# The seam between an inverse transform and a gated feed-forward: moving one transpose and one small transform, and moving one PSUM copy from ScalarE to VectorE

## The chip, the cores and the metric

The kernel runs on one core of one Trainium2 chip. The metric is device time in microseconds (us). Each execution also has a profiled span, from the first to the last instruction, which is about 1.8 us shorter. TensorE multiplies matrices into PSUM, which this kernel uses as 8 banks of 512 fp32 values per partition; ScalarE (ACT) and VectorE (DVE) move results from PSUM to SBUF ("evict" them; in the traces here 128x578 took 0.66 us on ScalarE); GpSimd (POOL) and SyncE (SP) start the transfers here, and GpSimd also computes ahead of the feed-forward (39.1 us busy in all, the DMA issues included).

## The reference

```python
def _A_ref(x, w_r, w_i):                     # spectral filter
    X = rfft2(x.astype(float32), axes=(-2, -1))
    y = irfft2(X * (w_r + 1j * w_i), s=(S, D), axes=(-2, -1)).astype(bfloat16)
    return y

def _B_ref(x, w_gate, w_up, w_down):         # gated feed-forward
    return (gelu(x @ w_gate) * (x @ w_up)) @ w_down

h  = x + _A_ref(layernorm(x), w_r, w_i)      # x: 1 x 2048 x 576, bf16
h2 = h + _B_ref(layernorm(h), w_gate, w_up, w_down)   # 576 -> 4608 -> 576
```

## The kernel before

The 2048 tokens are 16 tiles of 128. The Fourier transforms are matmuls with tables. The stage that matters is the last of the inverse transform and the start of the feed-forward. I name its pieces by token tile c:

- **I(c)**: six matmuls of 289 columns (three per PSUM bank, two banks), then the eviction into `GS`.
- **N(c)**: four matmuls of 288 columns, the last inverse transform; VectorE then adds the residual and sums the row for the next layernorm.
- **turn(k)**: the feed-forward wants the normalized tokens of the first block (tiles 0 to 3) with features on partitions. TensorE transposes each tile with five 128-column matmuls against an identity into two PSUM banks; one copy of 640 columns takes it to `HT0`.
- **gate/up**: 2592 matmuls of 512 columns that contract over only 64 rows (I call these half-height; all the others above are full-height, with 128 rows). They go in pairs, one on the upper and one on the lower half of the array, with the lower half six matmuls behind. The first six, `gu(0)`, therefore run alone; I call them the lone six. In the chain of waits of the kernel before, 648 paired ones take 70.05 us, 0.108 each, and the lone six 1.40, 0.233 each.

```python
TURN = (8, 10, 12, 14)            # after which tiles the four turns come

def islot(c):                     # I(c) uses PSUM banks 0,1 or 2,3
    return (c + sum(c > t for t in TURN)) % 2

def i_ev(c):
    sl, b0 = c % 2, 2 * islot(c)
    if c == 0:
        ...
    else:                         # one ScalarE instruction evicts both banks
        P.op(ACT, ... a.activation(GS[:, sl, :, 0:K2], banks(b0, 2, K2), ACTF.Copy),
             r=[("PS", b0), ("PS", b0 + 1)], w=[("G", sl, 0), ("G", sl, 1)])

def turn_pe(c):
    b0 = 2 * ((TURN[c] + 1 + c) % 2)        # the other pair of banks
    for k in range(5):
        ... PE matmul: HN tile x identity -> bank b0 + k // 4
    P.op(ACT, ... a.activation(HT0[:, 0:5, t0:t1], PS[... 640 columns from b0 ...], ACTF.Copy),
         r=[("PS", b0), ("PS", b0 + 1)], w=[("HT", 0, c, 0)])

st_I01()
for c in range(1, NT):
    if c >= 2:
        st_I(c)                   # six matmuls and i_ev(c)
    st_N(c - 1)
    ...                           # layernorm of tiles 0 to 3 at c = 5, 6, 7
    if c in TURN:
        turn_pe(TURN.index(c))
...
def gu(n):                        # gate/up, one step
    ...                           # n = 0: the lone six
    if n - 1 < 0:
        st_N(NT - 1)              # N15 comes inside the gate/up stream
        ...
```

A small scheduler in the kernel derives every semaphore wait from the `r` and `w` keys. A turn takes the pair of banks that would have been next, so the tile after a turn, I(c+1), uses the *same* banks as I(c). The kernel gives each engine its instructions as one list, in program order.

## Time and profile before

| | before |
|---|---|
| time, median of 3 first runs | 504.44 us (504.13 to 504.98) |
| profiled span | 502.9 us |
| TensorE busy | 98% |
| gate/up in the chain of waits | 56% |
| down projection in the chain of waits | 28% |

These are the first line of the engine table and the two lines of the chain on the profile's page. The chain follows the work that ended last back from the end; the shares are of the span.

```profile
PE 492.4 (98%) x4318; PEld 297.7 (59%) x4319; DVE 183.9 (37%) x391; ACT 158.7 (32%) x296; POOL 39.1 (8%) x49
...
PE 91%; DVE 6%; issue 1%; DMA 1%; ACT 1%; DVEq 0%
PE PS L838 56%; PE PS L861 28%; PE PS L700 3%; DVE TP L629 2%; PE PS L739 2%; PE PS L600 1%; DVE ST L440 1%; DVE CUS L606 1%; PE PS L645 1%; DVE CUS L607 1%; DMA XO<-in_A_x_dram 1%; PE PS L620 1%; DVE U L505 0%; DVE ATS L472 0%; ACT JNK L431 0%
```

The kernel is bound by TensorE: it is busy for 98% of the span, at a mean granted clock of 1.000 in the trace, and 91% of the chain lies on it. Below is the chain of waits of the kernel before, in order of time, around the seam. The columns are: start in us, length in us, engine, what is written, source line, and count. L700 is I, L739 is N, L784 is a turn, L838 is gate/up, L861 is the down projection. The first line is I8, the last I ahead of the first turn. In the experiments' kernels the line numbers shift by a few with each edit: I stays L700, N is L739 or L742, a turn L784 or L787, gate/up lies between L838 and L848.

```profile
65.15 0.75 PE PS L700 x6
...
72.49 0.90 PE PS L700 x6
73.39 0.49 PE PS L739 x4
73.88 0.75 PE PS L700 x6
74.63 0.49 PE PS L739 x4
75.12 0.28 PE PS L784 x5
75.40 0.90 PE PS L700 x6
76.30 0.49 PE PS L739 x4
76.79 1.40 PE PS L838 x6
78.19 0.60 PE PS L739 x4
78.79 70.05 PE PS L838 x648
148.84 35.39 PE PS L861 x288
```

TensorE is on the chain at every moment here, yet the same six matmuls take 0.75 us in one place and 0.90 in another (I13 at 72.49 and I15 at 75.40, both after a turn), and the same four take 0.49 or 0.60 (N15, inside the gate/up stream). A "busy" TensorE hides small waits, because the records of successive matmuls overlap: in the down projection successive matmuls of 288 columns start 0.123 us apart (288 in 35.39) and are each recorded as 0.286 long.

The timeline of the kernel before shows the wait. Its columns are: start, length, engine, line, operation, tiles, shape, count, and in brackets the idle time before it with what ended that.

```profile
74.67 0.66 ACT L709 ACTIVATE GS<-PS 128x578 bf16<-128x578 f32 x1 [0.59 <-PE PS L700]
...
74.96 0.44 PE L784 MATMUL PS<-IDT,HN 128*128 128x128 bf16 x5
...
75.38 0.92 PE L700 MATMUL PS<-DT,V 128*128 128x289 bf16 x6
...
76.34 0.66 ACT L709 ACTIVATE GS<-PS 128x578 bf16<-128x578 f32 x1 [0.19 <-PE PS L700]
...
78.12 0.67 PE L739 MATMUL PS<-GS,IT 128*128 128x288 bf16 x4
```

ScalarE evicts I14 from 74.67 to 75.33, and I15 begins at 75.38, although the turn ahead of it needs only 0.28 us from 74.96. On the other side, I15's own eviction (76.34 to 77.00) is long over when N15 begins at 78.12: the lone six hide it.

### The profile page before, as it was taken

Reading aid. Unit: us, or ns where it says so; the run is one execution under the profiler, and the core shown is the slowest. Engines: PE = TensorE matmul, PEld = TensorE weight load, DVE = VectorE, ACT = ScalarE, POOL = GpSimd, SP = SyncE. Lnnn points to the kernel's source line nnn. Section 1 sums busy time; section 2 is a strip of 40 time slices with the busy share of each in tenths; the row PEclk is TensorE's granted clock in tenths of the full one; section 3 lists DMA queues with packets and bytes.
Section 4 is the critical chain, followed back from the end, with each engine's and each line's share of the span. In section 5 each row is a group of like instructions: output and inputs, shape, how many; then the busy total and the mean of one; then the engine's idle time right before and its main releaser. Section 6 shows DMA issues by size and latency. Waiting matters only on the chain.

```text
span 502.9 us, 9972 instructions
## 1 busy us (share of the span) xinstructions
PE 492.4 (98%) x4318; PEld 297.7 (59%) x4319; DVE 183.9 (37%) x391; ACT 158.7 (32%) x296; POOL 39.1 (8%) x49
## 2 busy tenths in 40 slices
PE   6899999999999999999999999999999999999998
PEld 2687674444458764444477744444577644444775
DVE  5899673344431114343310134333201233333111
ACT  7888776653220003333200023323100133323000
POOL 3644281000000000000000000000000000000000
PEclk9999999999999999999999999999999999999999
DMA  8779789001100000100000001100000000000000
GB/s 284 165 224 334 235 292 353 6 4 25 25 5 13 18 19 17 22 17 1 2 7 18 19 15 23 22 4 1 1 18 19 13 1 1 1 2 2 12 19 19
DMA packets 25948, 28.64 MB, mean 57 GB/s; under 512 B 11568, under 2 KB 19888, under 8 KB 25776
## 3 DMA queue, kind: packets, MB, share of 16 engines
q1 hardware_dynamic: 23328, 17.39, 12.1%
q0 software_dynamic: 2576, 10.62, 6.3%
q8 instruction: 34, 0.56, 0.5%
q14 instruction: 10, 0.08, 0.1%
HBM read 23.66 MB, written 2.36 MB: 52 GB/s over the span
## 4 chain that ended last, share of the span: by engine, by line
PE 91%; DVE 6%; issue 1%; DMA 1%; ACT 1%; DVEq 0%
PE PS L838 56%; PE PS L861 28%; PE PS L700 3%; DVE TP L629 2%; PE PS L739 2%; PE PS L600 1%; DVE ST L440 1%; DVE CUS L606 1%; PE PS L645 1%; DVE CUS L607 1%; DMA XO<-in_A_x_dram 1%; PE PS L620 1%; DVE U L505 0%; DVE ATS L472 0%; ACT JNK L431 0%
## 5 line engine op out<-in xcount | busy, mean ns | idle before, releaser
L838 PE MATMUL PS<-HT,WGU 64*128 64x512 bf16 x2592 | 281.9, 376 | 0.0
L838 PEld LDWEIGHTS PS<-HT,WGU 64*128 64x128 bf16 x2592 | 137.3, 94 | 143.4 <-issue 1.2
L850 ACT ACTIVATE GL<-PS 128x512 bf16<-128x512 f32 x144 | 85.9, 597 | 289.3 <-PE PS L838 289.3
L851 DVE TENSOR_TENSOR AT<-GL,PS 128x512 bf16<-128x512 bf16 x144 | 99.0, 688 | 174.1 <-PE PS L838 172.5
L861 PE MATMUL PS<-WD,AT 128*128 128x288 bf16 (+2 forms) x1152 | 141.8, 286 | 0.0
L861 PEld LDWEIGHTS PS<-WD,AT 128*128 128x128 bf16 x1152 | 111.0, 98 | 31.5 <-issue 1.7
L864 DVE TENSOR_TENSOR OS<-PS,XO 128x288 bf16<-128x288 f32 (+2 forms) x32 | 14.7, 458 | 125.8 <-PE PS L861 125.8
L665 POOL TENSOR_SCALAR WS<-WS 128x290 bf16<-128x290 bf16 x16 | 15.2, 949 | 9.3 <-DMA WS<-in_A_w_i_dram 8.2
L742 DVE SCALAR_TENSOR_TENSOR XO<-PS,XO 128x576 bf16<-128x576 f32 x16 | 12.1, 756 | 8.4 <-PE PS L739 8.4
L645 PE MATMUL PS<-VT,ZS 128*128 128x256 bf16 x96 | 13.4, 272 | 1.7 <-DVE ZS L631 1.4
L600 PE MATMUL PS<-FT,U 128*128 128x290 bf16 x96 | 14.4, 287 | 0.5 <-DVE U L505 0.5
L700 PE MATMUL PS<-DT,V 128*128 128x289 bf16 x96 | 14.6, 287 | 0.2 <-DVE V L651 0.2
L629 DVE TENSOR_TENSOR TP<-YS,WS 128x580 bf16<-128x580 bf16 (+2 forms) x34 | 13.5, 438 | 0.3 <-issue 0.3
L656 ACT ACTIVATE V<-PS 128x768 bf16<-128x768 f32 x15 | 12.2, 811 | 2.1 <-PE PS L645 1.8
L623 ACT ACTIVATE YS<-PS 128x578 bf16<-128x578 f32 x16 | 10.5, 655 | 3.3 <-PE PS L620 3.3
L494 PE MATMUL PS<-ATS,XO 128*128 128x128 bf16 (+1 forms) x80 | 7.1, 223 | 4.4 <-POOL ATS L467 2.7
L709 ACT ACTIVATE GS<-PS 128x578 bf16<-128x578 f32 x15 | 9.8, 655 | 4.2 <-PE PS L700 4.1
L645 PEld LDWEIGHTS PS<-VT,ZS 128*128 128x128 bf16 x96 | 8.1, 97 | 4.8 <-DVE ZS L631 1.0
L600 PEld LDWEIGHTS PS<-FT,U 128*128 128x128 bf16 x96 | 9.2, 98 | 3.0 <-issue 0.7
L700 PEld LDWEIGHTS PS<-DT,V 128*128 128x128 bf16 x96 | 8.9, 97 | 3.4 <-DVE V L651 0.4
L730 ACT ACTIVATE OS<-XO 128x576 bf16<-128x576 bf16 x16 | 10.8, 675 | 0.0
L620 PE MATMUL PS<-CUS,BT 128*128 128x289 bf16 (+2 forms) x96 | 10.7, 247 | 0.0
(58 smaller groups left out, 158.6 us busy)
## 6 DMA issues: line engine op xcount, KB each, us to landing
WD<-in_B_w_down_dram POOLq DMA_DIRECT2D x9, 576.0 KB, 8.3
WGU<-in_B_w_up_dram SPq DMA_DIRECT2D x4, 1152.0 KB, 9.6
WGU<-in_B_w_gate_dram POOLq DMA_DIRECT2D x4, 1152.0 KB, 10.4
out_dram<-OS SPq DMA_DIRECT2D x30, 72.0 KB, 1.6
XO<-in_A_x_dram SPq DMA_DIRECT2D x3, 576.0 KB, 6.9
IT<-c_itab SPq DMA_DIRECT2D x1, 1024.0 KB, 7.0
HT<-HN SPq DMA_TRANSPOSE x60, 2.4
XO<-in_A_x_dram SPq DMA_DIRECT2D x2, 288.0 KB, 3.2
```

Source lines behind the costliest of these rows:

```text
L600: P.op(PE, lambda t, b=b, o=o, dt=dt, us=us, g=g: t.matmul(bank(b, 0, 128, 0, 2 * HK), U[:, us, g, :, :], FT[:, o, dt, :], start=(dt == 0) ...
L620: P.op(PE, lambda t, b=b, tb=tb, pl=pl, q0=q0, q1=q1, m=m, s3=s3, sp_=sp_: t.matmul(bank(b, 0, 128, q0, q1), BT[:, sp_, tb, :], CUS[:, s3, ...
L629: P.op(DVE, lambda v, sl=sl, g=g, q0=q0, q1=q1, t_=t_, w_=w_: v.tensor_tensor(TP[:, sl, t_, :, q0:q1], YS[:, sl, :, q0:q1], WS[:, g, w_, q ...
L645: P.op(PE, lambda t, b=b, o=o, c=c, zp=zp, sl=sl, sp_=sp_: t.matmul(bank(b, 0, 128, o, o + 256), ZS[:, sl, zp, 128 * c:128 * c + 128], VT[ ...
L656: P.op(ACT, lambda a, g=g, src=src: a.activation(V[:, :, :, g, :], src, ACTF.Copy), r=[("PS", bs[0]), ("PS", bs[2]), "Vfree"], w=[("V", g, ...
L665: P.op(POOL, lambda v, g=GORD[i]: v.tensor_scalar(WS[:, g, 0, :], WS[:, g, 2, :], -1.0, None, op0=ALU.mult), r=[k for k in wkeys[0 if 1 <= ...
L700: P.op(PE, lambda t, b=b, h=h, i=i, kt=kt, c=c: t.matmul(bank(b, 0, 128, 0, K2), V[:, kt, c, :, :], DT[:, 3 * h + i, 0:K2], start=(i == 0) ...
L838: op = P.op(PE, lambda t, h0=h0, kt=kt, wt=wt, f=f, b=b, HT=HT, s=(half == 0 and j in (0, 5)), e=(half == 1 and j in (3, 8)): t.matmul(ban ...
L850: P.op(ACT, lambda a, s2=s2, b0=b0: a.activation(GL[:, s2, :], bank(b0), ACTF.Gelu_apprx_tanh), r=[("PS", b0)], w=[("GL", s2)])
L851: P.op(DVE, lambda v, s2=s2, b0=b0, f=f: v.tensor_tensor(AT[:, f, :], GL[:, s2, :], bank(b0 + 1), op=ALU.mult), r=[("GL", s2), ("PS", b0 + ...
L861: P.op(PE, lambda t, b=b, d0=d0, d1=d1, f=f, p=p: t.matmul(bank(b, 0, 128, 0, d1 - d0), AT[:, f, 128 * p:128 * p + 128], WD[:, f, d0:d1], ...
L864: P.op(DVE, lambda v, b=b, d0=d0, d1=d1, p=p, c=c: v.tensor_tensor(OS[:, p % 2, d0:d1], bank(b, 0, 128, 0, d1 - d0), XO[:, c, d0:d1], op=A ...
```

## The change

The intent: let the fourth turn come after I15 and let N15 come directly after N14, ahead of the gate/up stream, so that nothing of the inverse transform stands inside that stream. The turn's copy goes to VectorE, because ScalarE is then busy with the eviction of I15 (0.66 us in the trace before).

```diff
-    TURN = (8, 10, 12, 14)
+    TURN = (8, 10, 12, 15)
@@ turn_pe
-        P.op(ACT, ... a.activation(HT0[:, 0:5, t0:t1], PS[...640 columns...], ACTF.Copy), ...)
+        src = PS[...640 columns...]
+        if c == 3:
+            P.op(DVE, ... v.tensor_copy(HT0[:, 0:5, t0:t1], src), ...)
+        else:
+            P.op(ACT, ... a.activation(HT0[:, 0:5, t0:t1], src, ACTF.Copy), ...)
@@ main loop
         if c >= 2:
             st_I(c)
+        if c == NT - 1:
+            turn_pe(3)
         st_N(c - 1)
 ...
-        if c in TURN:
+        if c in TURN[0:3]:
             turn_pe(TURN.index(c))
+    st_N(NT - 1)
@@ gu(0)
-            st_N(NT - 1)
```

TensorE's order in the seam goes from I14, N13, turn, I15, N14, lone six, N15, gate/up to I14, N13, I15, turn, N14, N15, gate/up. No matmul is added or removed. With no turn between I14 and I15, I15 has the other pair of banks.

More of the change, by code (lines that the diff above doesn't have):

```diff
@@ L785, in turn_pe @@
                  r=[("HN", hs, 0), ("HN", hs, 1), "IDT"], w=[("PS", b)])
-        P.op(ACT, lambda a, t0=t0, t1=t1, b0=b0: a.activation(HT0[:, 0:5, t0:t1], PS[:, b0 * 512:b0 * 512 + 640].rearrange("p (k e) -> p k e", k=5), ACTF.Copy),
-             r=[("PS", b0), ("PS", b0 + 1)], w=[("HT", 0, c, 0)])
+        src = PS[:, b0 * 512:b0 * 512 + 640].rearrange("p (k e) -> p k e", k=5)
+        if c == 3:
+            P.op(DVE, lambda v, t0=t0, t1=t1, src=src: v.tensor_copy(HT0[:, 0:5, t0:t1], src), r=[("PS", b0), ("PS", b0 + 1)], w=[("HT", 0, c, 0)])
+        else:
+            P.op(ACT, lambda a, t0=t0, t1=t1, src=src: a.activation(HT0[:, 0:5, t0:t1], src, ACTF.Copy), r=[("PS", b0), ("PS", b0 + 1)], w=[("HT", 0, c, 0)])
     st_I01()
```

## The prediction

> **What bounds the kernel.** TensorE. In the engine table it is busy 492.4 us of the 502.9 us span (98%), at full granted clock in every slice; the chain of waits lies 91% on it (gate/up matmuls 56% of the span, down projection 28%). The change touches only the seam between the inverse transforms and the gate/up stage. The timeline has there, by first starts on TensorE:
>
> I14 (six inverse matmuls, token tile 14) 73.72, N13 (four n1 matmuls) 74.47, fourth turn (five 128-wide transposes) 74.96, I15 75.38, N14 76.14, six lone gate/up matmuls 76.72, N15 78.12, steady gate/up stream 78.72.
>
> In the chain the groups cost: I 0.75 us (0.90 after a turn), N 0.49, turn 0.28, the lone six 1.40, N15 after them 0.60.
>
> **What changes.** The matmuls keep number and size. New order: I14, N13, I15, turn, N14, N15, gate/up.
>
> Gains on the critical path:
> 1. I15 follows a turn today and uses the PSUM banks of I14, so it waits for ScalarE's eviction of I14 (74.67 to 75.33; I15 begins at 75.38). Afterwards it has the other two banks: about -0.15.
> 2. N15 no longer splits the gate/up stream. It costs 0.60 there against 0.49 elsewhere, and the lone six take 1.40 [...]. Two changes between full-height and half-height matmuls vanish: -0.1 to -0.25.
>
> Losses on the critical path:
> 3. N15 had 1.4 us of gate/up work more between I15 and itself, which hid ScalarE's eviction of I15 (0.66). Now only turn and N14 (0.77) lie between. I15 starts at 74.96, is complete about 75.87, its eviction ends about 76.57; N15 could start at 76.48 but starts about 76.62: +0.1 to 0.15, a new wait on ScalarE.
> 4. Gate/up needs the turned tile. The 128x640 copy on VectorE should take 0.80 us (estimate from its PSUM copies of 256 columns, 0.425, and 512, 0.675), against 0.704 on ScalarE. It begins about 76.19 and ends about 76.99; N15 holds TensorE until about 77.11, so it is just hidden. On ScalarE it would queue with the I15 eviction; that is why it moves.
>
> The lone six then start about 77.20 and the steady stream about 78.48, against 78.72: -0.24 us. VectorE's N14 and N15 residual adds slide behind the copy, to about 78.7; their banks are wanted only later in gate/up, and those tiles' statistics later still. The Gelu table load still comes before the first Gelu. Everything after is the same instruction stream, so the shift should arrive whole at the end.
>
> **Predicted time: 504.2 us (-0.24 us, 0.05%), 8 in 10 between 503.6 and 504.8.** The three runs of before spread over 0.85 us, more than the effect. Faster by over 2%: 0.003; within 2%: 0.99; slower: 0.007.
>
> **What would show it.** In the timeline: I15 takes 0.75 directly after N13; a VectorE copy of 128x640 near 0.80 us; a gap of about 0.1 us before N15 that ends with ScalarE's eviction of I15; none before gate/up; the steady stream about 0.24 us earlier; its four blocks still 70.05 and 35.4 us each in the chain. Profiled span near 502.7.
>
> **What would make it wrong.** The copy ending after N15 [...] would make gate/up wait and cancel the gain; the wait on the I15 eviction could be larger; or splitting the stream costs less than I read, and the result is nil.

Two passages are cut from it, where marked. One is a term of the sum: the length of the lone six without the two changes, whose figure was not worked out from a trace. The sum came to -0.24 us and contains that term, between the two starts at 77.20 and 78.48; the upper end of its -0.1 to -0.25 rested on it too. An estimate that the trace before does give: 648 paired matmuls take 70.05 us, 0.216 a pair, and if one alone takes as long as a pair, six take 1.30; with that the sum is -0.22.

## The result, and the profile after

| | before | after |
|---|---|---|
| time, median of 4 | 504.71 us (504.13 to 505.09) | 504.40 us (503.95 to 504.82) |
| ratio | | 0.9995, 95% interval 0.9977 to 1.0012 |
| profiled span | 502.9 us | 502.3 us |
| I8 to the first down projection | 83.69 us | 83.48 us |

The verdict by rounds is "same" (only a difference of 2% or more counts as faster or slower). The ratio is the mean time of one kernel's fast runs over that of the other's of the same rounds, so it is not quite the ratio of the medians. By timing alone the two kernels are the same.

The last row is the measure I use from here on. The spans differ by 0.6 us, but 0.37 us of that lies ahead of I8 (65.15 against 64.78), in a part of the program where the two kernels have the same instructions in the same order. The stretch from the begin of I8 to the begin of the first down projection contains everything that the change touches. The chain of waits of the changed kernel (the line numbers of later code are 5 or 6 higher: L844 is gate/up, L866 the down projection):

```profile
64.78 0.75 PE PS L700 x6
...
73.51 0.75 PE PS L700 x6
74.26 0.49 PE PS L739 x4
74.76 0.75 PE PS L700 x6
75.50 0.28 PE PS L784 x5
75.78 1.13 PE PS L739 x8
76.92 71.34 PE PS L844 x654
148.26 35.38 PE PS L866 x288
```

Read against the lines of before, I15 fell from 0.90 to 0.75 us. Gate/up is one piece of 71.34, which is the 70.05 of the paired stream and 1.29 for the lone six, instead of 1.40. N14 and N15 together take 1.13, where they took 0.49 + 0.60 = 1.09; without any wait they would take 2 x 0.49 = 0.98, so there is a new wait of 0.15. The sum is -0.15 - 0.11 + 0.04 = -0.22, and the stretch moved by -0.21.

The timeline of the changed kernel names the new wait:

```profile
75.34 0.44 PE L784 MATMUL PS<-IDT,HN 128*128 128x128 bf16 x5
...
75.54 0.65 ACT L709 ACTIVATE GS<-PS 128x578 bf16<-128x578 f32 x1 [0.59 <-PE PS L700]
...
75.62 1.30 PE L739 MATMUL PS<-GS,IT 128*128 128x288 bf16 x8
75.82 0.82 DVE L788 CAST HT<-PS 128x640 bf16<-128x640 f32 x1 [0.26 <-PE PS L784]
...
76.25 0.36 PEld L739 LDWEIGHTS PS<-GS,IT 128*128 128x128 bf16 x4 [0.28 <-ACT GS L709]
...
76.85 3.42 PE L844 MATMUL PS<-HT,WGU 64*128 64x512 bf16 x24
```

The weight load of N15 (line `PEld L739`) waits for the eviction of I15, which ends at 76.19. The VectorE copy of the turn ends at 76.64, and gate/up begins at 76.85.

### The profile page after: what moved, and what is told of

Same layout as the page of the kernel before. It is cut to its first block, busy times and chain, and to the rows that moved or that the text cites. A ratio compares the mean times of both kernels' runs of the same rounds, so it can differ in the third digit from the quotient of the medians.

```text
span 502.3 us, 9974 instructions
## 1 busy us (share of the span) xinstructions
PE 493.7 (98%) x4319; PEld 299.4 (60%) x4319; DVE 184.2 (37%) x392; ACT 158.1 (31%) x295; POOL 39.3 (8%) x49
## 4 chain that ended last, share of the span: by engine, by line
PE 89%; DVE 7%; issue 2%; ACT 1%; DMA 1%; DVEq 0%
PE PS L844 56%; PE PS L866 28%; PE PS L700 2%; DVE TP L629 2%; PE PS L739 2%; DVE ST L440 1%; DVE CUS L606 1%; DVE CUS L607 1%; DMA XO<-in_A_x_dram 1%; PE PS L600 1%; DVE ATS L472 0%; ACT JNK L431 0%; DVE ZS L631 0%; PE PS L784 0%; ACT U L507 0%
## 5 line engine op out<-in xcount | busy, mean ns | idle before, releaser
L844 PE MATMUL PS<-HT,WGU 64*128 64x512 bf16 x2592 | 281.8, 376 | 0.0
L844 PEld LDWEIGHTS PS<-HT,WGU 64*128 64x128 bf16 x2592 | 138.0, 94 | 142.8 <-issue 0.9
L866 PE MATMUL PS<-WD,AT 128*128 128x288 bf16 (+2 forms) x1152 | 141.8, 286 | 0.0
L866 PEld LDWEIGHTS PS<-WD,AT 128*128 128x128 bf16 x1152 | 111.0, 98 | 31.5 <-issue 1.7
L739 PE MATMUL PS<-GS,IT 128*128 128x288 bf16 x64 | 10.5, 285 | 0.0
```

Of the source, the lines that this page charges most:

```text
L739: P.op(PE, lambda t, b=b, h=h, i=i, c=c, rhs=rhs: t.matmul(bank(b, 0, 128, 0, 288), IT[:, h * i, c, :], rhs, start=(i == 0), stop=(i == 1) ...
L844: op = P.op(PE, lambda t, h0=h0, kt=kt, wt=wt, f=f, b=b, HT=HT, s=(half == 0 and j in (0, 5)), e=(half == 1 and j in (3, 8)): t.matmul(ban ...
L866: P.op(PE, lambda t, b=b, d0=d0, d1=d1, f=f, p=p: t.matmul(bank(b, 0, 128, 0, d1 - d0), AT[:, f, 128 * p:128 * p + 128], WD[:, f, d0:d1], ...
```

## The experiments

Nine kernels were run (before, changed, and seven edits), all correct. The kernel before repeated, N15 alone, the turn alone, the copy on ScalarE and the split eviction of I15 were given one profiled execution each ("one look"), whose state is therefore unknown; no conclusion here rests on their times, only on the stretch inside the trace. Rounds give a ratio to the kernel before, run on the same chip. The traces of the experiments come from three chips (12, 14 and 15), and the kernel before was traced again on chip 14 alone. The pieces that no edit touches have the same length in every trace (I without a wait 0.75 us, N 0.49, a paired gate/up block 70.05, within 0.01), so I compare the stretches across chips.

### Does the stretch repeat at all? Both kernels again

No edit: the kernel before again, and the changed kernel again.

> The kernel before, profiled again. Measure for all runs: in the chain of waits, from the begin of I8 (six inverse matmuls of token tile 8, ahead of the first turn) to the begin of the first down projection; it was 83.69 us before (65.15 to 148.84) and 83.48 us after (64.78 to 148.26). My theory: this stretch is fixed by the instruction order, so it repeats within 0.03 us (83.69), while the begin of I8 wanders by some tenths of a us from execution to execution. Rival (all of the difference is chance): the stretch wanders by 0.1 to 0.3 us too.

> The changed kernel again. My theory: stretch from I8 to the first down projection 83.48 us within 0.03, time 0.2 us under the kernel before, which five rounds can hardly resolve (ratio 0.9995, interval of about plus or minus 0.001). Rival (chance): the stretch is anywhere between 83.4 and 83.8.

The kernel before (one look) began I8 at 65.86 and its first down projection at 149.55: 83.69 us. The changed kernel ran from 64.68 to 148.16: 83.48 us. Both repeat to the last digit. The begin of I8 is what wanders: over all eleven traces it lay between 64.45 and 65.86, a spread of 1.4 us, more than six times the effect. Five rounds gave a ratio of 0.9996 (0.9982 to 1.0009), as blind as the first comparison. The rival, that the whole difference is chance, falls: 0.21 us belongs to the change, and the 0.37 us by which the changed kernel was ahead when it reached I8 does not.

### N15 moved alone

Kernel before, with only this:

```diff
         if c in TURN:
             turn_pe(TURN.index(c))
+    st_N(NT - 1)
@@ gu(0)
-            st_N(NT - 1)
```

> Kernel before with only N15 moved ahead of the gate/up matmuls; the fourth turn stays after N13, on ScalarE. My theory: the eviction of I15 is no longer hidden; N15 begins 1.66 us after I15, as it did in the changed kernel, and so waits about 0.42 us after N14; I15 still costs 0.90. Stretch 83.90 us, 0.21 longer than before: a loss. Rival (the gain is that N15 no longer splits the gate/up stream, the turn is incidental): 83.45 to 83.50, a gain of 0.2.

The stretch was 149.20 - 65.30 = 83.90 us: 0.21 longer than before. The chain of waits of this kernel leaves TensorE at the seam:

```profile
75.55 0.91 PE PS L700 x6
76.46 0.02 issue
76.48 0.66 ACT GS L709
77.15 0.04 issue
77.19 0.67 PE PS L739 x4
77.86 71.34 PE PS L839 x654
```

N15 stands still until ScalarE has evicted I15. N14, the only work left to cover that eviction, is too short. The lone six cost 1.29 here too (71.34 - 70.05), so the gain of an unsplit stream is real (0.11 on the lone six and 0.11 on N15), but alone it is paid for with a wait of about 0.42.

### The turn moved alone

Changed kernel, with N15 put back into `gu(0)`:

```diff
-    st_N(NT - 1)
@@ gu(0)
+            st_N(NT - 1)
```

> Changed kernel with only N15 put back into the gate/up stream; the fourth turn stays after I15 with its copy on VectorE. My theory: I15 costs 0.75, but then only N14 lies between the turn and gate/up, and the copy (0.82 us) is not hidden: gate/up begins 3.34 us after I14 instead of 3.00. Stretch 84.03 us, 0.34 longer than before: a loss. Rival (only the splitting of the stream matters): 83.69, as before, or 83.55 with I15 at 0.75.

The stretch was 149.16 - 65.05 = 84.11 us: 0.42 longer than before. Its chain of waits:

```profile
75.02 0.75 PE PS L700 x6
75.77 0.29 PE PS L784 x5
76.06 0.02 issue
76.09 0.83 DVE HT L788
76.92 0.14 issue
77.06 1.45 PE PS L843 x6
78.51 0.60 PE PS L739 x4
```

I15 costs 0.75, as the theory has it, but the copy on VectorE now stands in the chain. The loss was 0.08 more than expected, and the line `76.92 0.14 issue` says where: gate/up begins 0.14 to 0.15 us after the copy's end, not the 0.05 that I had taken from I15 after I14's eviction.

So each half of the change is a loss by itself (+0.21 and +0.42), and the two together are a gain of 0.21. N15 covers the turn's copy, and the turn helps to cover I15's eviction.

### The engine of the copy

Changed kernel with the fourth copy back on ScalarE:

```diff
-        if c == 3:
+        if c == 4:                # never true: ScalarE for all four turns
             P.op(DVE, ... tensor_copy ...)
```

> Changed kernel with the copy of the fourth turn on ScalarE, as it was. My theory: it comes behind the eviction of I15 (ends 2.84 us after I14), takes 0.70 and ends 3.57; gate/up begins 3.62 after I14 instead of 3.50. Stretch 83.60 us, 0.12 more than the changed kernel but still 0.09 less than before. Rival (the engine of the copy does not matter, N15 hides it): 83.48.

The stretch was 148.00 - 64.45 = 83.55 us: 0.07 more than the changed kernel. ScalarE began the copy at 75.77, took 0.70 and ended at 76.47; gate/up began at 76.61. The expected +0.12 was the sum of two errors: I had the copy end 3.57 us after the first matmul of I14, and it ended at 3.44 (I14 began at 73.03), since ScalarE starts it 0.11 ahead of the recorded end of the eviction; and I had gate/up follow 0.05 later, where it followed 0.14 later. The direction held: VectorE is the better engine here, although its copy takes 0.82 us and ScalarE's 0.70, because ScalarE gets to the copy only after the eviction of I15. The choice of engine is worth a third of the total gain.

### The eviction of I15 in two pieces

Changed kernel, with

```diff
+        elif c == NT - 1:
+            for h in range(2):     # one ScalarE instruction per PSUM bank
+                P.op(ACT, ... a.activation(GS[:, sl, h, 0:K2], bank(b0 + h, ...), ACTF.Copy),
+                     r=[("PS", b0 + h)], w=[("G", sl, h)])
         else:                      # one instruction for both banks
```

> Changed kernel with only the eviction of I15 cut into one ScalarE instruction per PSUM bank. My theory: the new wait ahead of N15 vanishes, N15 begins 2.76 us after I14 instead of 2.90, gate/up 3.36 instead of 3.50, with the VectorE copy (ends 3.29) now about level with it. Stretch 83.34 us, 0.14 less than the changed kernel. Rival (N15 waits for something else than this eviction, or the copy already sets the begin of gate/up): 83.45 to 83.48.

The stretch was 148.86 - 65.45 = 83.41 us: 0.07 less than the changed kernel, half of what I expected. These are the two chain lines:

```profile
76.45 0.99 PE PS L742 x8
...
77.46 71.40 PE PS L847 x654
```

N14 and N15 together fell from 1.13 to 0.99, so the wait ahead of N15 did vanish. But the VectorE copy (76.49 to 77.31) then set the begin of gate/up at 77.46, again 0.15 after its end. In the changed kernel the copy ends at 76.64, and 0.15 later is 76.79: it was hidden with only 0.06 us to spare.

### The same for every tile beside a turn

Changed kernel, with the condition above as `elif c in TURN` (tiles 8, 10, 12 and 15).

> Changed kernel with ScalarE's eviction of an inverse tile beside a turn (token tiles 8, 10, 12, 15) cut into one instruction per PSUM bank, so that the next matmuls wait for the first bank only. My theory: I9, I11, I13 after a turn take 0.75 to 0.78 instead of 0.90 us, N15 no longer waits for the eviction of I15 (0.14), the copy of the fourth turn on VectorE then ends just as N15 does. Stretch 82.9 us, 0.58 less than the changed kernel, 0.8 less than before; time about 503.8 against 504.6. Rival (two instructions cost ScalarE 0.84 instead of 0.66 us, and that delays the turn copies or the next evictions as much): 83.4 to 83.6.

The stretch was 147.63 - 64.67 = 82.96 us, 0.52 less than the changed kernel. The time over five rounds was 503.49 us (503.32 to 504.10) against 504.55 for the kernel before, ratio 0.9981 (0.9968 to 0.9993). The interval leaves out 1. Four of its chain lines:

```profile
65.91 0.28 PE PS L787 x5
66.19 0.75 PE PS L700 x6
...
76.21 0.02 issue
76.23 71.40 PE PS L847 x654
```

I9 takes 0.75 directly behind a turn; I11 and I13 do too. That is 3 x 0.15, and with the 0.07 of the split at I15 it makes the 0.52; the expected 0.58 had again left out the time between the copy's end and gate/up. Two evictions of one bank take 0.414 us each, as the one-bank eviction of tile 0 did in the kernel before (L707), instead of 0.655 for both banks in one, so ScalarE works longer in total (0.79 from the begin of the first to the end of the second), but the first bank is free earlier, and that is what TensorE waits for.

### The copy shared by two engines

The kernel just above, and

```diff
-            P.op(DVE, ... v.tensor_copy(HT0[:, 0:5, t0:t1], src), r=[("PS", b0), ("PS", b0 + 1)], ...)
+            P.op(DVE, ... v.tensor_copy(HT0[:, 0:4, t0:t1], src[:, 0:4, :]), r=[("PS", b0)], w=[("HT", 0, c, 0)])
+            P.op(ACT, ... a.activation(HT0[:, 4, t0:t1], src[:, 4, :], ACTF.Copy), r=[("PS", b0 + 1)], w=[("HT", 0, c, 1)])
```

> The kernel with split evictions beside the turns, and the copy of the fourth turn shared: VectorE the 512 columns of the first PSUM bank (0.675 us, from the earlier copies), ScalarE the 128 of the second. My theory: in the split kernels gate/up begins 0.15 us after the end of the 0.82 us copy, so the copy sets it; shared, N15 sets it again, 0.09 us earlier. Stretch from I8 to the first down projection 82.87 us instead of 82.96. Rival (the 0.15 is a fixed cost of going from the n1 matmuls to gate/up, whatever the copy): 82.96, unchanged. Time about 503.4 to 503.9, not told apart from the split kernel by rounds.

The stretch was 147.89 - 65.00 = 82.89 us, another 0.07 less. These are the two pieces in the timeline, and the begin of gate/up:

```profile
75.54 0.69 DVE L791 CAST HT<-PS 128x512 bf16<-128x512 f32 x1 [0.21 <-PE PS L787]
75.62 0.27 ACT L792 ACTIVATE HT<-PS 128x128 bf16<-128x128 f32 x1
...
76.47 2.34 PE L848 MATMUL PS<-HT,WGU 64*128 64x512 bf16 x14
```

The copy ends at 76.23 and gate/up begins 0.24 later, where it began 0.14 to 0.15 after the copies that it waited for; and in the chain gate/up now follows N15 directly. So it no longer waits for the copy: TensorE's own matmuls set the begin. Five rounds gave 503.53 us (503.23 to 503.84) against 504.43, ratio 0.9983 (0.9971 to 0.9996). Rounds do not tell this kernel from the one above; the stretch does. By the stretch these two are the fastest, ahead of both the kernel before and the changed one. By rounds both intervals against the kernel before leave out 1, with a difference far under 2%; no ratio to the changed kernel was taken.

### The cause without the move

Kernel before, order unchanged, the copy on ScalarE, only the evictions of tiles 8, 10, 12 and 14 split in two as above.

> Kernel before, order unchanged, only ScalarE's evictions of token tiles 8, 10, 12 and 14 cut into one instruction per PSUM bank. My theory: the 0.15 us that an inverse group loses after a turn is the wait on the eviction of the tile before in the same banks; with it cut, all four groups after turns take 0.75, gate/up still costs 1.40 and N15 0.60. Stretch 83.09 us, 0.60 less than before and 0.39 less than the changed kernel, without moving anything. Rival (the 0.15 comes from going from the transposes to the inverse matmuls): 83.69.

The stretch was 147.99 - 64.89 = 83.10 us: 0.59 less than before and 0.38 less than the changed kernel.

```profile
74.42 0.28 PE PS L787 x5
74.70 0.75 PE PS L700 x6
...
75.94 1.40 PE PS L841 x6
77.34 0.60 PE PS L742 x4
```

I15 follows the turn and takes 0.75. The rival, that going from transposes to inverse matmuls costs 0.15 by itself, falls. The rest of the seam (1.40, 0.60) is as before. Five rounds: 503.92 us (503.53 to 504.23) against 504.43, ratio 0.9991 (0.9977 to 1.0004).

| kernel | I8 to down projection, us | against before |
|---|---|---|
| before (twice) | 83.69, 83.69 | |
| changed (twice) | 83.48, 83.48 | -0.21 |
| only N15 moved | 83.90 | +0.21 |
| only the turn moved | 84.11 | +0.42 |
| changed, copy on ScalarE | 83.55 | -0.14 |
| changed, I15 eviction split | 83.41 | -0.28 |
| before, four evictions split | 83.10 | -0.59 |
| changed, four evictions split | 82.96 | -0.73 |
| the same, copy shared | 82.89 | -0.80 |

## Why the prediction was right

The prediction was 504.2 us, -0.24; the median measured was 504.40, and the stretch moved by -0.21. The time by itself shows little: the predicted range was 503.6 to 504.8, and the medians of the kernel before (504.44 and 504.71) lie in it too, so a change worth nothing would have landed there as well. What bears the prediction out is the trace. Counted from the first matmul of I14, it put N15 at 2.90 us and gate/up at 3.48; the timeline has 2.90 (76.25 - 73.35) and 3.50 (76.85 - 73.35). Point by point:

1. **I15 without its wait, about -0.15.** Right: 0.90 to 0.75 in the chain. That the cause is ScalarE's eviction from shared banks is shown by the kernel before with split evictions, which removes the 0.15 without moving anything. The wait itself follows from the program: I15 writes the banks that the eviction of I14 reads, and the scheduler orders the two by their keys; no run here dropped it. That one instruction over two banks holds both until it ends is the doing of this kernel's scheduler, which hangs both keys on that instruction.
2. **N15 out of the stream, -0.1 to -0.25.** Right, at the upper end: the lone six went from 1.40 to 1.29 and N15 from 0.60 to 0.49 without its wait, 0.11 each. Before, the seam had three changes between full-height and half-height matmuls, after it has one, so the 0.22 went with two changes. What the 0.11 consists of was not shown; no run here took it apart. The trace allows one inference: at each of the three changes before, the first weight load begins together with the first matmul (76.72, 78.12 and 78.72 in the timeline), where for N14 it begins 0.13 ahead (76.01 and 76.14). A weight load is recorded at 0.09 to 0.10 us, so a load that is not hidden would by its length account for most of the 0.11.
3. **A new wait on the eviction of I15, +0.1 to +0.15.** Right: 1.13 - 0.98 = 0.15 in the chain, named by the weight load that waited for it, and removed by splitting the eviction (0.99).
4. **The copy on VectorE, 0.80 us and just hidden.** Right in outcome. The duration was 0.82; the 0.80 was an estimate from two VectorE copies in the trace before (256 columns in 0.425 us at L651, 512 in 0.675 at L505). On ScalarE the same 640 columns took 0.704 (L786 in the trace before). The margin was mis-sized: I had the copy end 0.12 us ahead of N15's end and counted no time between the copy and gate/up, where the runs show that gate/up begins 0.15 after the copy. That left 0.06 us, not 0.12. The outcome was unaffected, but the error returned in three later expectations (the turn moved alone, the I15 eviction split, and that split at every tile beside a turn). The time from the end of an eviction to the first matmul that waited for it was 0.05 to 0.06 us with the same matmul form (I15 after I14's eviction, 75.33 to 75.38 before; N15 after I15's, 76.19 to 76.25 after), and 0.14 to 0.15 where the waiting matmul is half-height and the one ahead of it full-height; what makes the difference was not tested.
5. **The rest unchanged.** Right: the paired stream is 70.05 us and the down projections 35.4 us each before and after, and the shift arrived whole at the end. VectorE's residual adds of N14 and N15 did slide behind the copy (76.56 to 77.98), and no wait in the trace is put down to them.

What the prediction did not see is that it described the smaller share of the loss. The same bank wait as at I15 stood behind the three earlier turns as well (0.90 at I9, I11 and I13), and it can be cut without reordering for 0.59 us in all.

Not settled: why the begin of I8 wanders by 1.4 us. In the slowest case (65.86) the three large loads of the input took a median of 7.5 us to land, in the fastest (64.45) 6.5, but the traces between do not follow (7.1 us with I8 at 64.68, 6.8 with I8 at 65.45). The granted clock between 12.5 and 25 us does not sort with it either: it was 0.86 in seven traces (I8 at 64.45 to 65.86) and 1.00 in four (64.67 to 65.30). Nothing was varied to test it.

## What to carry to other kernels

Here a move on an engine that was 98% busy freed one wait (0.15 us at I15) and uncovered another (0.15 ahead of N15), so list for each consumer what used to cover its producer; either half of the change lost time (0.21 and 0.42 us) and only both together gained (0.21). When a group of identical matmuls takes longer in some places than in others (here 0.90 against 0.75 us), look for one eviction that spans several banks in front of it, and try to cut it per bank before reordering anything; here that alone gave 0.59 us, where reordering gave 0.21. When the effect is smaller than the scatter of the time, compare a stretch of the trace between two points that enclose the change: here it repeated to 0.01 us while the start of the stretch wandered by 1.4 us.
